# Handing out six PSUM banks by expected release, and moving the middle of an output unit of a fused attention and MLP kernel

## The chip, the cores and the metric

The kernel runs on one core of one Trainium2 chip. Its time is what the device takes for one execution, in microseconds (us); the figure given for a kernel is the median of its runs. One further execution was profiled. All readings below are of that one.

## The reference

The input is `x`, 2048 tokens of 576 features, in float32. Two branches are computed from it and mixed by a gate, one value for each token.

```
qkv = x @ wqkv                       # 32 heads of 18
p = softmax(q k^T * 18**-0.5)        # 2048 x 2048 for each head
a = (p @ v) @ wo
y = layernorm(x)                     # no scale, no shift
b = gelu_tanh(y @ w1 + b1) @ w2 + b2 # 576 -> 4608 -> 576
g = sigmoid(sum(x * gate_w))
out = g * a + (1 - g) * b
```

## The kernel before, in words

The order of the instructions on each engine is the order in which the program writes them; nothing reorders them later. Nearly every float32 product is made of three float32r products, of a high and a low part of each operand.

**Opening.** The tokens are transposed on TensorE (`transposed`, L909), projected to q, k and v (`qk_group` L994, `v_group` L1012), and stored. The normed tokens are transposed too (`y_chunk`). In the gaps of this order stand the first maxima (below).

**The loop.** Attention runs by 32 units. A unit is one pair of heads and one half of the queries. It has 16 steps, one for each 128 keys, so the loop has 512 steps. Head 0 of a pair lies in rows 0 to 63 of TensorE's array and head 1 in rows 64 to 127, so that two matmuls, one on each half of the array, can run side by side. Three sorts of attention work are in the loop:

- *Maxima* (`s1_round`, L227 and L229). A matmul of 128 queries by 512 keys, and on VectorE a maximum over it. One round is two matmuls, one for each head. There are 32 rounds a unit, done for the unit after the current one. `s1_finish` makes of them rows that are stored into the query tile by eight small DMAs (`qa<-mr`).
- *Scores for exp* (`s2`, L310 and L312). A matmul of 128 keys by 512 queries, with the negated maximum as extra rows, and the exponential on ScalarE. A call of `s2` is two matmuls, one for each head. Each step has two calls.
- *Sums* (`pv`, L338). The exponentials times the values, four narrow matmuls side by side, accumulated in one PSUM bank over the 16 steps of a unit. `pv` is called once in two or three steps. At a unit's end VectorE copies the bank out (`oe`, L351).

The MLP branch is a generator, `mlp`, that the loop draws from between two calls of `s2` (`fill`, which takes one `atom`, up to the next cut). It has two kinds of pieces. `h_pair` makes two blocks of the hidden layer, 27 pairs of matmuls of 512 columns (L582), of which the GELU is made on ScalarE, VectorE and GpSimd. `out_pair` makes one *output unit*: 24 pairs of matmuls of 288 columns (L714, 64 rows each) for 128 tokens, whose two results VectorE adds to an accumulator (L688). There are 144 output units.

In the first twelve pairs of an output unit, the *first turn*, array half 0 adds into one bank and half 1 into the other. In the second turn the halves change banks. Before the first product of the second turn the program waits on the semaphore `turn`, which the last products of the first turn raise. The middle of the unit is this place.

A call of `s2` takes a round of maxima with it where `loop_round` gives one: the order is then score, maximum, maximum, score, on halves 0, 1, 0, 1. Where it gives none, its two matmuls are *woven* (`weave`) with the MLP's: score on half 0 beside two MLP products on half 1, and then the reverse. `lend_round` takes a round ahead of its call, as two maxima alone, and marks in `lent` that the next call goes without. `next_round` does a round that no call owes.

**PSUM.** Of the eight banks of 512 float32 columns, two (`ps_w`) belong to the MLP. Two (`ps_s2`) belong to the scores for exp, by turns. Four (`ps_x`) are shared by maxima and sums: three go round for the maxima (`Rotating`, which the opening's transposes use too), and one holds the running sum; when a new sum begins, `Sums` takes the next of the three and gives back the old one.

Of the kernel before, what the change touches and what calls it, by code (L numbers as in the profile page):

```python
# [29 lines left out]
G = 4  # L30
# [23 lines left out]
AHEAD = 3200.0  # L54
BARE = NSTEP - LEAD - NT
# [5 lines left out]
def gated_mix_kernel(ctx: ExitStack, tc: tile.TileContext, x, wqkv, wo, w1, b1, w2, b2, gate_w, out):  # L61
# [37 lines left out]
    class Rotating:  # L99
# [6 lines left out]
    class Sums:  # L106

        def tile(self, *args, **kw):
            i = turn_x.pop(0)
            turn_x.append(held_x[0])  # L110
            held_x[0] = i
            return ps_x[i].tile(*args, **kw)

    ps_s1 = Rotating()
    ps_o = Sums()
# [100 lines left out]
    def s1_round(u, r):  # L216


        t, kb = (r % 8, r // 8) if u == 0 else divmod(r, 4)
        if r == 0:  # L220
            M4[u] = asm.tile([P, 2, 8, 4], F32, name="m4")
        qa, ka = QA[u % 3], k_tile(UNITS[u][0])

        def head(h):
            r0 = 64 * h
            ps = psum(ps_s1)
            nc.tensor.matmul(ps, qa[r0:r0 + 54, t * P:(t + 1) * P], ka[r0:r0 + 54, kb * TB:(kb + 1) * TB],  # L227
                             start=True, stop=True)
            nc.vector.tensor_reduce(M4[u][:, h, t, kb:kb + 1], ps, axis=AX.X, op=ALU.max)  # L229
        return head  # L230
# [53 lines left out]
    def weave(order, heads, need):  # L284

        if not held:
            for h in order:
                heads[h]()
            return
# [9 lines left out]
    def s2(u, kc, qb, around, ns):  # L299
# [7 lines left out]
        def head(h):  # L307
            ps = psum(ps_s2)
# [3 lines left out]
            nc.scalar.activation(ring(n)[:, qb, h], ps, AF.Exp, scale=SCALE)  # L312

# [13 lines left out]
    def pv(n0, n1):  # L327

        flush()
        for c in range(n0, n1):  # L330
            u, k = divmod(c, NT)
            if k == 0:
                OB[u] = psum(ps_o)
            v = VT[UNITS[u][0] % 2]
            for qb in range(2):
                for h in range(2):
                    r = 32 * (2 * h + qb)
                    nc.tensor.matmul(OB[u][r:r + 32, :], v[:, k, 19 * h:19 * h + 32], ring(c)[:, qb, h, :],  # L338
                                     start=(k == 0), stop=(k == NT - 1))
            if k == NT - 1:  # L340
                o_store(u, OB.pop(u))
# [4 lines left out]
    def o_store(u, ps):  # L346
# [4 lines left out]
        nc.vector.tensor_copy(oe, ps)  # L351
        cols = slice(2 * pair * DH, 2 * (pair + 1) * DH)
# [53 lines left out]
    def mlp():  # L406
# [63 lines left out]
        def split(table, key, pool, shape, raw, src, scr, then):  # L470

            def first():
# [3 lines left out]
                nc.scalar.activation(t[:, 0], src(), AF.Copy)  # L476
                bg.insert(0, (any_time, lambda: second(t), queue))
# [64 lines left out]
        def free_pool():  # L542

            if rounds:
                return ps_w
            turns[0] += 1
            return (ps_s1, ps_w)[(turns[0] - 1) // 2 % 2]

        def banks(q):

            if q % 2 and not looped[0]:
                return [psum(ps_s2) for _ in range(2)]
            return [psum(free_pool()) for _ in range(2)]

        def h_pair(q, last, inner=False):
# [8 lines left out]
            ps = banks(q)  # L564
# [14 lines left out]
            for k, (w_, s_, c) in enumerate(slots):  # L579
# [3 lines left out]
                weave((0, 1), [partial(head, 0), partial(head, 1)], 1)  # L583
# [23 lines left out]
            nc.scalar.activation(zs[0], ps[0], AF.Identity, bias=b[0])  # L607
            for h in (1, 0):
# [52 lines left out]
                def second(w, parts):  # L661
                    aside[0] = slot[0]
                    nc.scalar.activation(w, w, AF.Tanh, scale=GC1)
                    if early:
# [3 lines left out]
                def square(w=w, z=z):  # L668
                    aside[0] = slot[0]
                    nc.scalar.activation(w, z, AF.Square)  # L670
                    if early:
# [6 lines left out]
        def out_pair(i, t, acc):  # L678
# [11 lines left out]
            ps = [psum(free_pool()) for _ in range(2)]  # L690
            ends = {7, 15} if piece[0] == 0 else cuts(24, max(1, 3 - piece[0]))
            k = 0
            for turn in range(2):
                if turn == 1:
                    flush()
                if turn == 1 and bare:
                    add(ps, g == 0)
                    ps = [psum(free_pool()) for _ in range(2)]
# [5 lines left out]
                for j in ORDER:  # L704
# [5 lines left out]
                    for h_, p_ in ((hh, 0), (hh, 1), (hl, 0)):  # L710
# [13 lines left out]
                        weave((0, 1) if turn == 0 else (1, 0), [partial(head, 0), partial(head, 1)], 2)  # L724
# [9 lines left out]
            add(ps, g == 0 and not bare)  # L734
            if g == NG - 1:
# [123 lines left out]
    with ExitStack() as a:  # L859
# [46 lines left out]
        def transposed(tb, c):  # L906
            ps = psum(ps_s1)
            for t in range(4):
                nc.tensor.transpose(ps[:, t * P:(t + 1) * P], x_view(tb)[:, t, c * P:(c + 1) * P], ident)  # L909
            return ps  # L910
# [119 lines left out]
        def v_chunk(tb, stage):  # L1030
# [16 lines left out]
            for c in cs_:  # L1047
                for cy in (c, 4 + c) if c < 4 else (8,):
                    ps = psum(ps_s1)
                    for t in range(4):  # L1050
                        nc.tensor.transpose(ps[:, t * P:(t + 1) * P], x_view(tb)[:, t, 64 * cy:64 * cy + P], ident)
                    nc.scalar.activation(made[0][:, cy, :], ps, AF.Copy)
# [22 lines left out]
        for tb in range(NB):  # L1075
# [3 lines left out]
            for g, (fn, args) in enumerate(work):  # L1079
# [49 lines left out]
                if tb == 2 and g == 13:  # L1129
                    ps = psum(ps_s1)  # L1130
                    nc.tensor.transpose(ps[:, :NFC], b1r, ident[:NFC, :NFC])
                    nc.vector.tensor_copy(b1t, ps[:, :NFC])
                for _ in range(ROUNDS[tb](g)):
# [7 lines left out]
    ps_s2 = ctx.enter_context(tc.tile_pool(name="ps_s2", bufs=2, space=PSUM))  # L1141
# [15 lines left out]
    def out_proj():  # L1157
# [125 lines left out]
        for b in range(NB):  # L1283
            per = 4 if b == 2 else 1
            res = {}
            for i0 in range(0, 8, per):
# [4 lines left out]
                for cut_ in (range(4), range(4, 5)):  # L1291
                    for t, n in tiles:
                        tok = slice(t * P, (t + 1) * P)
                        cs = slice(n * ND, (n + 1) * ND)
                        if 0 in cut_:
                            ps[t, n] = psum((ps_s1, ps_w)[banks % 2])
                            banks += 1
                        for c in cut_:
# [3 lines left out]
                            flush()  # L1302
                            for k, (s_, w_) in enumerate(prods):
# [7 lines left out]
                        if n == 0:  # L1311
                            res[t] = io.tile([P, D], F32, name="res")
                        nc.vector.scalar_tensor_tensor(res[t][:, cs], ps[t, n][:, :ND], gate[:, tt:tt + 1], BT[tt // 2][:, t % 2, cs],
                                                       op0=ALU.mult, op1=ALU.add)
                        yield 122.5
# [113 lines left out]
```

## Time and profile before

| what | us |
|---|---|
| median of three runs (range) | 2239.19 (2237.62 to 2239.44) |
| the profiled execution | 2240.08 |
| its span, from the first to the last instruction | 2238.3 |
| TensorE (PE) busy | 2222.0 |
| VectorE (DVE) busy | 1651.7 |
| ScalarE (ACT) busy | 1440.2 |
| GpSimd (POOL) busy | 949.1 |

The profiled execution took 1.8 us more than its span, and lies 0.9 us above the median. PE is busy through nearly the whole span, but this share must be read with care: a matmul counts as busy from its start to a modelled end, and matmuls on the two halves of the array overlap. A half that stands still while the other one works, or while the last product drains, shows as no idle time. So the starts of matmuls are what is to be read here, against the pace at which they follow each other where nothing holds them up.

### The profile page before, as it was taken

How to read it: one execution, taken by the hardware profiler on the slowest of the kernel's cores; microseconds unless marked ns; L12 is line 12 of the kernel's file. 1: busy time of each engine (PE TensorE's matmuls, PEld its weight loads, DVE VectorE, ACT ScalarE, POOL GpSimd, SP SyncE). 2: the span in 40 equal slices, each digit the busy share in tenths (PEclk: the TensorE clock that was granted, in tenths of full speed). 3: DMA queues.
4: the chain of work that ended last, by engine and by line, in shares of the span. 5: the costliest groups of instructions: out<-in, count | busy, mean ns of one | idle time of the engine just before them, and what ended most of it. 6: DMA issues, size and time to landing. Idle time of an engine off the chain costs nothing.

```text
span 2238.3 us, 51156 instructions
## 1 busy us (share of the span) xinstructions
PE 2222.0 (99%) x20569; PEld 1619.8 (72%) x20569; DVE 1651.7 (74%) x2887; ACT 1440.2 (64%) x2719; POOL 949.1 (42%) x936
## 2 busy tenths in 40 slices
PE   8999999999999999999999999999999999999999
PEld 7878677777767776677776776776777677777668
DVE  5675777777777777777777777777777777787834
ACT  4223677777776666666666666666766667666771
POOL 4002466666664444444445444444534444434420
PEclk9999999999999999999999999999999999999999
DMA  7755654536485424242273424233563333333355
GB/s 237 259 190 181 204 171 140 168 133 177 149 228 184 123 100 122 99 143 96 99 184 138 123 99 123 100 125 119 138 182 113 133 114 102 113 93 105 122 175 179
DMA packets 163411, 323.62 MB, mean 145 GB/s; under 512 B 59838, under 2 KB 86370, under 8 KB 152338
## 3 DMA queue, kind: packets, MB, share of 16 engines
q1 hardware_dynamic: 159462, 313.60, 44.0%
q10 hardware_dynamic: 3712, 6.75, 0.8%
q8 instruction: 162, 2.65, 0.5%
q14 instruction: 75, 0.61, 0.1%
HBM read 229.07 MB, written 95.16 MB: 145 GB/s over the span
## 4 chain that ended last, share of the span: by engine, by line
PE 96%; DVE 1%; DMA 1%; POOL 1%; ACT 1%; SPq 0%; issue 0%; ACTq 0%; DVEq 0%; POOLq 0%
PE ps L338 21%; PE ps L714 20%; PE ps L582 20%; PE ps L310 14%; PE ps L227 11%; PE ps L994 5%; PE ps L1012 2%; PE ps L1304 2%; PE ps L909 1%; PE ps L1043 0%; DMA x<-in_A_x_dram 0%; DVE m L229 0%; POOL zz L180 0%; DMA ot_scr<-dn_scr 0%; DMA dn_scr<-dn 0%
## 5 line engine op out<-in xcount | busy, mean ns | idle before, releaser
L229 DVE TENSOR_REDUCE m<-ps 128x1 f32<-128x512 f32 x2048 | 1302.7, 684 | 327.1 <-PE ps L227 273.5
L312 ACT ACTIVATE p<-ps 128x512 f32<-128x512 f32 x1080 | 586.7, 596 | 290.7 <-PE ps L227 185.4
L310 PE MATMUL ps<-qa,ka 56*128 56x512 f32 x2048 | 701.0, 411 | 3.2 <-DMA qa<-mr 2.6
L312 ACT ACTIVATE ring<-ps 128x512 f32<-128x512 f32 x968 | 525.8, 596 | 270.9 <-PE ps L227 175.9
L227 PE MATMUL ps<-ka,qa 54*128 54x512 f32 x2048 | 648.5, 415 | 1.2 <-DVE big L925 0.8
L714 PE MATMUL ps<-w,hh 64*128 64x288 f32 x4352 | 530.3, 296 | 0.7 <-ACT z L607 0.6
L582 PE MATMUL ps<-big,w 64*128 64x512 f32 x3888 | 516.4, 392 | 0.1
L310 PEld LDWEIGHTS ps<-qa,ka 56*128 56x128 f32 x2048 | 360.8, 185 | 213.3 <-issue 75.0
L180 POOL TENSOR_SCALAR zz<-zz 128x512 f32<-128x512 f32 x272 | 169.1, 622 | 759.3 <-ACT zz L670 730.3
L582 PEld LDWEIGHTS ps<-big,w 64*128 64x128 f32 x3888 | 379.4, 185 | 74.8 <-ACT vt L1023 0.3
L714 PEld LDWEIGHTS ps<-w,hh 64*128 64x128 f32 x4352 | 421.1, 186 | 14.2 <-ACT z L607 1.0
L180 POOL TENSOR_TENSOR zz<-zz,z 128x512 f32<-128x512 f32 x280 | 361.8, 1292 | 36.5 <-ACT zz L672 10.5
L714 PE MATMUL ps<-w,hl 64*128 64x288 f32 x2176 | 363.5, 292 | 0.0
L227 PEld LDWEIGHTS ps<-ka,qa 54*128 54x128 f32 x2048 | 339.4, 185 | 29.3 <-DVE m L229 5.7
L338 PE MATMUL ps<-p,vt 128*32 128x512 f32 x2160 | 265.2, 598 | 0.1
L714 PEld LDWEIGHTS ps<-w,hl 64*128 64x128 f32 x2176 | 248.4, 185 | 1.1
L338 PE MATMUL ps<-ring,vt 128*32 128x512 f32 x1936 | 238.3, 598 | 0.0
L180 POOL TENSOR_TENSOR w<-x,w 128x576 fp32r<-128x576 f32 (+1 forms) x34 | 68.4, 2013 | 273.8 <-ACT w L476 247.7
L180 POOL TENSOR_TENSOR hl<-zz,hh 128x512 fp32r<-128x512 f32 x134 | 174.3, 1301 | 15.2 <-ACT hh L633 4.4
L688 DVE SCALAR_TENSOR_TENSOR x<-ps,x 128x288 f32<-128x288 f32 x268 | 110.1, 453 | 85.7 <-PE ps L714 76.9
L338 PEld LDWEIGHTS ps<-p,vt 128*32 128x32 f32 x2160 | 57.9, 109 | 127.0 <-issue 125.4
L338 PEld LDWEIGHTS ps<-ring,vt 128*32 128x32 f32 x1936 | 52.1, 109 | 112.9 <-issue 112.7
(120 smaller groups left out, 1470.0 us busy)
## 6 DMA issues: line engine op xcount, KB each, us to landing
w<-w_scr SPq DMA_DIRECT2D x54, 1152.0 KB
w<-w_scr SPq DMA_DIRECT2D x108, 576.0 KB
w_scr<-w SPq DMA_DIRECT2D x18, 1152.0 KB
w_scr<-w SPq DMA_DIRECT2D x36, 576.0 KB
qa<-qk_scr SPq DMA_DIRECT2D x192, 72.0 KB
ka<-qk_scr SPq DMA_DIRECT2D x90, 144.0 KB
big<-y_scr SPq DMA_DIRECT2D x48, 256.0 KB
x<-in_B_w_dram SPq DMA_DIRECT2D x34, 288.0 KB
```

The costliest lines, as they stand in the source:

```text
L180: fn(*args, **kw)
L227: nc.tensor.matmul(ps, qa[r0:r0 + 54, t * P:(t + 1) * P], ka[r0:r0 + 54, kb * TB:(kb + 1) * TB], start=True, stop=True)
L229: nc.vector.tensor_reduce(M4[u][:, h, t, kb:kb + 1], ps, axis=AX.X, op=ALU.max)
L310: nc.tensor.matmul(ps, ka[r0:r0 + 56, kc * P:(kc + 1) * P], qa[r0:r0 + 56, qb * TB:(qb + 1) * TB], start=True, stop=True)
L312: nc.scalar.activation(ring(n)[:, qb, h], ps, AF.Exp, scale=SCALE)
L338: nc.tensor.matmul(OB[u][r:r + 32, :], v[:, k, 19 * h:19 * h + 32], ring(c)[:, qb, h, :], start=(k == 0), stop=(k == NT - 1))
L582: nc.tensor.matmul(ps[h], wt[w_][r, c, :], Y[s_][r, c, :], start=(k == 0), stop=(k == 26))
L688: nc.vector.scalar_tensor_tensor(dst, ps[nn][:, :ND], 0.5, b2b[:, cs[nn]] if base else dst, op0=ALU.mult, op1=ALU.add)
L714: mm = nc.tensor.matmul(ps[nn][:, :ND], h_[r, tok], w_[p_][r, cs[nn]], start=(k == 0 or bare and k == 3 * G), stop=(k == 6 * G - 1 or bare ...
L994: nc.tensor.matmul(ps, w_[:, c, ms], big[:, s_, :], start=(k == 0), stop=(k == len(prods) - 1))
L1012: nc.tensor.matmul(ps[:, :ND], big[:, s_, tok], w_[:, c, cs], start=(k == 0), stop=False)
L1304: nc.tensor.matmul(ps[t, n][:, :ND], OT[b][3][:, s_, tok], w_part(w_, c)[:, cs], start=(c == 0 and k == 0), stop=(c == 4 and k == 1))
```

## The change

The program keeps a rough clock for PE, ACT and DVE while it is written out. Six banks (four `ps_x`, and two more once the loop begins) are one pool. A matmul for scores, maxima or sums, and in some places a pair of the MLP's, takes the bank whose release is expected first (`Earliest`). After the reading instruction is written, `let_go` sets when that bank is expected back: the reader's clock, plus a fixed time. `ps_w` stays. In the opening the pool has four banks, all of them in use.

In an output unit that begins at a cut (`piece[0] == 0`) while rounds of maxima remain, here `folded`, the cuts fall behind pairs 6 and 12 in place of 7 and 15. The first cut's call of `s2` goes without maxima, the second one's call, with maxima, falls on the middle, so that no round is lent there. The round that the first call passed over is done alone behind pair 18. (Each of the first four output units has one round more, as before.)

```diff
+DRAIN = 330.0
+MAX_NS = 580.0
+EXP_NS = 490.0
...
-    ps_x = [ctx.enter_context(tc.tile_pool(name=f"ps_x{i}", bufs=1, space=PSUM)) for i in range(NS1 + 1)]
-    turn_x = list(range(NS1))
-    held_x = [NS1]
...
+    bank_x = [ctx.enter_context(tc.tile_pool(name=f"ps_x{i}", bufs=1, space=PSUM)) for i in range(4)]
+    free_at = [0.0] * 4
+    pe_t, act_t, dve_t = [0.0], [0.0], [0.0]
+
+    class Earliest:
+
         def tile(self, *args, **kw):
-            i = turn_x.pop(0)
-            turn_x.append(i)
-            return ps_x[i].tile(*args, **kw)
+            i = min(range(len(bank_x)), key=lambda b: free_at[b])
+            pe_t[0] = max(pe_t[0], free_at[i])
+            taken[0] = i
+            free_at[i] = 1e12
+            return bank_x[i].tile(*args, **kw)
...
+    def let_go(i, clock, ns):
+
+        clock[0] = max(clock[0], pe_t[0] + DRAIN) + ns
+        free_at[i] = clock[0]
...
             nc.vector.tensor_reduce(M4[u][:, h, t, kb:kb + 1], ps, axis=AX.X, op=ALU.max)
+            pe_t[0] += 116.0
+            let_go(taken[0], dve_t, MAX_NS)
...
             nc.scalar.activation(ring(n)[:, qb, h], ps, AF.Exp, scale=SCALE)
+            pe_t[0] += 116.0
+            let_go(taken[0], act_t, EXP_NS)
...
         nc.vector.tensor_copy(oe, ps)
+        let_go(bank, dve_t, 620.0)
...
             ends = {7, 15} if piece[0] == 0 else cuts(24, max(1, 3 - piece[0]))
+            folded = piece[0] == 0 and not bare
+            if folded:
+                ends = {6, 12}
...
                     if 3 * G not in ends:
                         lend_round()
                     turned[0] += 2
                     nc.tensor.wait_ge(turn_sem, turned[0])
...
-                        if k == 5 * G and extra[0]:
-                            extra[0] -= 1
+                        if folded and k == 6:
+                            if extra[0]:
+                                extra[0] -= 1
+                            else:
+                                lent[0] = 1
+                        if folded and k == 18:
                             next_round()
...
-    ps_s2 = ctx.enter_context(tc.tile_pool(name="ps_s2", bufs=2, space=PSUM))
+    for i in range(4, 6):
+        bank_x.append(ctx.enter_context(tc.tile_pool(name=f"ps_x{i}", bufs=1, space=PSUM)))
+        free_at.append(pe_t[0])
```

**On PE.** The first piece is an output unit as 134 of the 144 stand in the program before, from the call behind pair 7 to a little past the middle. L714 is a product of the output unit, L310 a score for exp, L227 a maximum; `ps` is the bank written, `w`, `hh` and `hl` are the MLP's operands.

```order
L310 MATMUL ps<-qa_111,ka_112 128x512 [waits Activation_49]
L227 MATMUL ps<-ka_112,qa_109 128x512 [waits DVE_49] x2
L310 MATMUL ps<-qa_111,ka_112 128x512 [waits Activation_49]
L714 MATMUL ps<-w_9841,hh 128x288 x2
L714 MATMUL ps<-w_9841,hl 128x288 x2
L714 MATMUL ps<-w_9839,hh 128x288 x4
L714 MATMUL ps<-w_9839,hl 128x288 x2
L227 MATMUL ps<-ka_112,qa_109 128x512 [waits DVE_49] x2
L714 MATMUL ps<-w_9835,hh 128x288 [waits turn]
L714 MATMUL ps<-w_9835,hh 128x288 x3
L714 MATMUL ps<-w_9835,hl 128x288 x2
```

The two lent maxima, and nothing else, stand between the last products of the first turn and the product that waits for them.

The second piece is the same place of a like unit in the changed program, where the lines have other numbers: L751 is the output unit's product, L320 the score, L234 the maximum.

```order
L751 MATMUL ps<-w_9236,w_8897 128x288 x6
L320 MATMUL ps<-qa_110,ka_113 128x512 [waits DVE_49]
L234 MATMUL ps<-ka_112,qa_111 128x512 [waits Activation_49]
L234 MATMUL ps<-ka_112,qa_111 128x512 [waits DVE_49]
L320 MATMUL ps<-qa_110,ka_113 128x512 [waits Activation_49]
L751 MATMUL ps<-w_9208,hh 128x288 [waits turn]
L751 MATMUL ps<-w_9208,hh 128x288 x3
L751 MATMUL ps<-w_9208,hl 128x288 x2
L751 MATMUL ps<-w_9223,hh 128x288 x4
L751 MATMUL ps<-w_9223,hl 128x288 x2
L234 MATMUL ps<-ka_112,qa_111 128x512 [waits Activation_49] x2
L751 MATMUL ps<-w_9251,w_8897 128x288 x6
```

Two scores and two maxima now stand at the turn, and the two maxima without scores have moved six pairs behind it, where no product waits for a semaphore. A score can now wait for DVE and a maximum for ACT, since banks pass from one kind to the other.

**On ACT.** The next two pieces are exponentials (L312, then L322) of the loop, each written into one of the ring's tiles (`p`, `ring`), with what they wait for. First the program before:

```order
L312 ACTIVATE p<-ps 128x512 [waits PE_49] x2
L663 ACTIVATE zz<-zz 128x512 [waits Pool_49]
L312 ACTIVATE p<-ps 128x512 [waits PE_49] x4
L312 ACTIVATE ring_2271<-ps 128x512 [waits PE_49] x4
L312 ACTIVATE p<-ps 128x512 [waits PE_49] x8
```

and the changed one:

```order
L322 ACTIVATE ring_2282<-ps 128x512 [waits PE_49] x4
L322 ACTIVATE p<-ps 128x512 [waits PE_49] x2
L322 ACTIVATE p<-ps 128x512 [waits PE_49,Activation_49]
L322 ACTIVATE p<-ps 128x512 [waits PE_49]
L322 ACTIVATE p<-ps 128x512 [waits PE_49,Activation_49]
L322 ACTIVATE p<-ps 128x512 [waits PE_49]
L322 ACTIVATE p<-ps 128x512 [waits PE_49,Activation_49] x2
```

Some exponentials (488 of 2048) have a second wait, for ACT's own earlier write of the same ring tile. Before, that was known from the score's wait for ACT; it no longer is where the score's bank came back from DVE.

More of the change, by code (lines that the diff above doesn't have):

```diff
@@ L282, in flush, with weave @@
             tail()
-    def weave(order, heads, need):
+    def weave(order, heads, need, ns):
+        pe_t[0] += ns
         if not held:
@@ L476, in first @@
                 nc.scalar.activation(t[:, 0], src(), AF.Copy)
+                engine(act_t, 900.0)
                 bg.insert(0, (any_time, lambda: second(t), queue))
@@ L540, in mlp, with pair_of_banks, wide_banks, give_back @@
         turns = [0]
[L542 to L547, printed above, removed]
+        def pair_of_banks(own):
+            if own:
+                return [psum(ps_w) for _ in range(2)], ()
+            tiles, ids = [], []
+            for _ in range(2):
+                tiles.append(psum(ps_x))
+                ids.append(taken[0])
+            return tiles, ids
         def banks(q):
             if q % 2 and not looped[0]:
-                return [psum(ps_s2) for _ in range(2)]
-            return [psum(free_pool()) for _ in range(2)]
+                return pair_of_banks(False)
+            return wide_banks()
+        def wide_banks():
+            if rounds:
+                return pair_of_banks(True)
+            turns[0] += 1
+            return pair_of_banks(turns[0] % 2 == 0)
+        def give_back(ids):
+            for b in ids:
+                let_go(b, dve_t, 480.0)
         def h_pair(q, last, inner=False):
@@ L563, in h_pair @@
             del W1[q]
-            ps = banks(q)
+            ps, ids = banks(q)
             if q == 0:
@@ L607, in h_pair @@
             nc.scalar.activation(zs[0], ps[0], AF.Identity, bias=b[0])
+            engine(act_t, 690.0)
+            give_back(ids)
             for h in (1, 0):
@@ L663, in second @@
                     nc.scalar.activation(w, w, AF.Tanh, scale=GC1)
+                    engine(act_t, 640.0)
                     if early:
@@ L670, in square @@
                     nc.scalar.activation(w, z, AF.Square)
+                    engine(act_t, 640.0)
                     if early:
@@ L697, in out_pair @@
                     add(ps, g == 0)
-                    ps = [psum(free_pool()) for _ in range(2)]
+                    give_back(ids)
+                    ps, ids = wide_banks()
                 elif turn == 1:
@@ L1284, in out_proj @@
             per = 4 if b == 2 else 1
-            res = {}
+            res, own = {}, {}
             for i0 in range(0, 8, per):
@@ L1295, in out_proj @@
                         if 0 in cut_:
-                            ps[t, n] = psum((ps_s1, ps_w)[banks % 2])
+                            ps[t, n] = psum((ps_x, ps_w)[banks % 2])
+                            own[t, n] = None if banks % 2 else taken[0]
                             banks += 1
@@ L1314, in out_proj @@
                                                        op0=ALU.mult, op1=ALU.add)
+                        if own[t, n] is not None:
+                            let_go(own[t, n], dve_t, 480.0)
                         yield 122.5
```

43 lines of the change are left out of this document (22 added, 21 removed).

## The prediction

> **What bounds the kernel now.** I read the page first, then the busy time in chosen stretches, then the starts of matmuls one by one.
>
> ```profile
> span 2238.3 us, 51156 instructions
> PE 2222.0 (99%) x20569; PEld 1619.8 (72%) x20569; DVE 1651.7 (74%) x2887; ACT 1440.2 (64%) x2719; POOL 949.1 (42%) x936
> ...
> PE 96%; DVE 1%; DMA 1%; POOL 1%; ACT 1%; SPq 0%; issue 0%; ACTq 0%; DVEq 0%; POOLq 0%
> ```
>
> The first two lines and the chain that ended last say that TensorE sets the time. They leave it 16 us of idle time in all, so that no wait seems worth removing. But busy is not the same as working, so I took one output unit and cut it at its middle. The columns after the stretch are its length, then busy time and instructions of each engine.
>
> ```profile
> core 0: us, PE busy (x) PEld busy (x) DVE busy (x) ACT busy (x) POOL busy (x), PEclk, DMA share, GB/s
> 805.84:807.90 2.06, 2.06 (x30) 2.04 (x27) 2.06 (x5) 1.74 (x4) 0.00 (x0) 1.00 0.10 19
> 807.90:810.68 2.78, 2.78 (x36) 2.50 (x32) 2.17 (x5) 1.62 (x4) 0.00 (x0) 1.00 0.45 125
> 1000.00:1500.00 500.00, 500.00 (x4936) 354.12 (x4934) 384.71 (x662) 337.97 (x646) 224.36 (x237) 1.00 0.39 125
> ```
>
> PE is busy for the whole of both halves, at full clock. The first half holds 12 product pairs, one score pair and one maxima pair. The second holds 12 product pairs, the lent maxima, a woven score pair, and a last call of two pairs. What these should take is read from the starts in that unit (timeline of PE alone: start, length, what):
>
> ```profile
> 805.60 0.40 PE L310 MATMUL ps<-qa,ka 56*128 56x512 f32 x1
> 805.84 0.43 PE L714 MATMUL ps<-w,hh 64*128 64x288 f32 x4
> ...
> 806.76 0.40 PE L227 MATMUL ps<-ka,qa 54*128 54x512 f32 x1
> ...
> 807.24 0.32 PE L714 MATMUL ps<-w,hh 64*128 64x288 f32 x2
> ...
> 807.90 0.39 PE L227 MATMUL ps<-ka,qa 54*128 54x512 f32 x1
> ...
> 807.98 0.49 PE L227 MATMUL ps<-ka,qa 54*128 54x512 f32 x1
> ...
> 808.16 0.40 PE L714 MATMUL ps<-w,hh 64*128 64x288 f32 x1
> 808.16 0.45 PE L714 MATMUL ps<-w,hh 64*128 64x288 f32 x2
> ...
> 810.36 0.39 PE L310 MATMUL ps<-qa,ka 56*128 56x512 f32 x1
> ...
> 810.68 0.64 PE L338 MATMUL ps<-p,vt 128*32 128x512 f32 x4
> ```
>
> From 805.84 to 806.76 stand seven product pairs: 0.92 / 7 = 0.131 us for one. From 806.76 to 807.24 stand two pairs of 512 columns: 0.24 us for one, as from 805.60 to 805.84. The sums (L338) begin 0.32 us after the last score, 0.08 more than its 0.24. So the first half should take 12 x 0.131 + 2 x 0.24 = 2.05 us, and takes 2.06. The second should take 12 x 0.131 + 4 x 0.24 + 0.08 = 2.61 us, and takes 2.78. The loss is all behind the turn. There the second maximum starts 0.08 us after the first (it waits for a bank that DVE has to read), the product with the wait on `turn` starts at 808.16, and the next product of the other half behind it. The first maximum left its half of the array free at about 807.90 + 0.24 = 808.14, with nothing to run until those products are let in.
>
> Is this one unit typical? These are the first product and the first sum of the three others of its group (the pair 805.84 and 810.68 above is the fourth):
>
> ```profile
> 791.08 0.43 PE L714 MATMUL ps<-w,hh 64*128 64x288 f32 x4
> ...
> 796.11 0.64 PE L338 MATMUL ps<-p,vt 128*32 128x512 f32 x4
> ...
> 798.54 0.43 PE L714 MATMUL ps<-w,hh 64*128 64x288 f32 x4
> ...
> 803.41 0.64 PE L338 MATMUL ps<-ring,vt 128*32 128x512 f32 x4
> ...
> 813.11 0.43 PE L714 MATMUL ps<-w,hh 64*128 64x288 f32 x4
> ...
> 817.98 0.64 PE L338 MATMUL ps<-ring,vt 128*32 128x512 f32 x4
> ```
>
> The four take 5.03, 4.87, 4.84 and 4.87 us, on the mean 4.90. Undisturbed, a unit is 24 x 0.131 + 6 x 0.24 + 0.08 = 4.66 us. The loss is 0.24 us on the mean, 0.18 at the least, 0.37 at the most.
>
> **The change part by part.**
>
> *The turn.* The orders of both programs have 134 output units of the one pattern, replaced by the other; work and number of `pv` calls are the same. In the new order the two array halves have 2 x 0.24 = 0.48 us of scores and maxima to stream between the last product of the first turn and the one that waits for it; before, they had one pair, 0.24 us, of which the second began late. In the row above the waiting product starts 0.26 us after the lent maxima do, so 0.48 us covers the wait with 0.2 to spare. What is queued behind this wait on PE is the whole kernel, so what it gives up is time. I take 0.20 us a unit: more than the least of the four, less than their mean, because the slowest (5.03) also has tanh passes on ACT, which stay. 134 x 0.20 = 26.8 us. The ends: nothing, if a new wait stands at the turn or at the moved maxima, and 134 x 0.24 = 32 us.
>
> *What is late next: the banks.* How long a bank is held is read where both readers were idle (start, length, engine):
>
> ```profile
> 999.02 0.39 PE L310 MATMUL ps<-qa,ka 56*128 56x512 f32 x1
> 999.03 0.62 PE L227 MATMUL ps<-ka,qa 54*128 54x512 f32 x2
> ...
> 999.45 0.60 ACT L312 ACTIVATE ring<-ps 128x512 f32<-128x512 f32 x1 [0.55 <-PE ps L227]
> 999.49 0.69 DVE L229 TENSOR_REDUCE m<-ps 128x1 f32<-128x512 f32 x1 [0.34 <-PE ps L227]
> ```
>
> A score holds its bank 1.03 us (to 1000.05), a maximum 1.15 us (to 1000.18). Now the new unit by the prices above, from its first product: call without maxima at 0.79, call at the turn at 1.81, lone maxima at 3.08, last call at 4.10 and 4.34, sums at 4.66. By the program's bank numbers the shortest reuse, at 1.26 us of distance, is of three kinds: a score at the turn takes the bank of the first woven score, the second lone maximum that of a score or a maximum at the turn, and the last score that of the first lone maximum. Against 1.03 us there are 0.23 to spare, against 1.15 only 0.11. Does DVE keep up?
>
> ```profile
> 806.01 3.72 DVE L229 TENSOR_REDUCE m<-ps 128x1 f32<-128x512 f32 x6
> 810.33 0.82 DVE L688 SCALAR_TENSOR_TENSOR x<-ps,x 128x288 f32<-128x288 f32 x2 [0.61 <-PE ps L714]
> ```
>
> Six maxima in a row take 3.72 us, 0.62 each. At the turn the first can start at 1.81 + 0.46 = 2.27, the second ends its turn by 2.27 + 2 x 0.62 = 3.51, and the lone ones are ready at 3.08 + 0.46 = 3.54: no queue. So the bank comes back at 3.08 + 1.15 = 4.23, and the last score wants it at 4.34. Cost: nothing, with 0.11 us of cover. If DVE lags by one maximum the wait is 0.62 - 0.11 = 0.51 us a unit (rivals).
>
> *The opening.* Here the order stays, and the ring of three banks becomes a pool of four. Two of the places where a maximum waits for a bank:
>
> ```profile
> 135.53 0.49 PE L227 MATMUL ps<-ka,qa 54*128 54x512 f32 x1
> ...
> 136.81 0.49 PE L227 MATMUL ps<-ka,qa 54*128 54x512 f32 x1 [0.79 <-DVE big L925]
> ...
> 141.19 1.09 PE L227 MATMUL ps<-ka,qa 54*128 54x512 f32 x2
> ...
> 141.79 0.18 PEld L227 LDWEIGHTS ps<-ka,qa 54*128 54x128 f32 x1 [0.42 <-DVE m L229]
> ```
>
> The second maximum starts 1.28 and 0.60 us after the first, on the other half of the array, which could start at once. With a fourth bank it takes one that was used a tile earlier. The most is 1.9 us; the least is nothing, if DVE's queue only passes the wait on. I take 1.5, nearer the upper end, since the first wait is for a transpose's reader (`big` L925) and not for DVE's queue of maxima.
>
> *ACT.* Of the exponentials 488 get a second wait. The nearest row is that of the GELU's first step, which has such waits:
>
> ```profile
> L607 ACTq EVENT_SEMAPHORE  x68: 17/17/38, 307.8 to 2113.9; - x68
> ```
>
> At 0.017 us each they come to 8.3 us of ACT's time. ACT is busy 338 of 500 us in the loop, so I cost them at nothing; if that cover is gone, all 8.3 us. Each makes a score's bank come back 0.02 us later, out of 0.23.
>
> *The maxima's lead.* The round passed over at the first cut comes later by up to one call; four calls and the sums stand in 7.30 us (805.84 less 798.54), so that is 1.8 us. Last maximum of a unit, its rows' DMAs, first score that needs them:
>
> ```profile
> 1880.66 0.57 PE L227 MATMUL ps<-ka,qa 54*128 54x512 f32 x2
> ...
> 1887.62 5.57 SPq L134 DMA_DIRECT2D qa<-mr  x8
> ...
> 1897.10 0.39 PE L310 MATMUL ps<-qa,ka 56*128 56x512 f32 x1
> ```
>
> The last DMA is issued by 1893.19, and 3.9 us are left to land. Less 1.8, and less what a faster loop takes from it (under 0.5), 1.6 us remain. These eight stay in their order on SP's queue, so a later maximum holds up what stands behind them there (loads of q, k, weights) by the same 1.8 us at most, ahead of uses that are whole units away. Cost: nothing; at the worst the rows land late by the 1.8 us for 31 units, 56 us, which the 3.9 us argue against.
>
> *DMAs, GpSimd, the other lines* are neither added nor removed.
>
> The sum, against the profiled execution: 2240.1 - 26.8 - 1.5 = 2211.8 us. The median of the runs is 0.9 us below that execution, so I give 2211.
>
> **The rivals.**
>
> *Half of it.* The turn is freed, but the lone maxima or the last score wait by about 0.10 us a unit, as the second lent maximum does now by 0.08. For it: the cover is only 0.11 us, and the program's clock for DVE leaves out the 0.82 us of the two additions. Against: these come before the maxima at the turn, and DVE is idle 115 of 500 us. 134 x 0.10 = 13.4 us gained, 1.5 in the opening: 2225.
>
> *Slower: exponentials wait for DVE.* Before, no score waited for DVE. Now the last score of a unit needs the bank of the first lone maximum. If DVE lags there by one maximum, 0.62 us, the wait is 0.51 us a unit, and 134 x (0.51 - 0.20) = 41.5 us are lost: 2280. It decides from a lag of 0.11 + 0.20 = 0.31 us on. For it: DVE works in the order written, so any GELU or softmax step in front adds its whole length. Against: such a step stands in the unit's first half or in hidden-layer stretches, and the additions leave DVE about 1 us free in a unit (8 x 0.62 + 0.82 = 5.78 of 7.30).
>
> *No change: the readers of PSUM are the pace.* If DVE and ACT empty the banks as fast as they can, a stall removed on PE comes back as a wait for a bank: 2240. For it: DVE is busy without a gap in the first half of the unit above (2.06 of 2.06). Against: 2.17 of 2.78 in the second, and 385 of 500 in the loop. The Trainium skill, "TensorEngine Tiling (Array Packing)", section "Performance Considerations", has this as a rule: tiling speeds up TensorE but not the emptying of PSUM, which may then become the bottleneck. By that rule the whole 28 us would not come. The trace agrees only for stretches of some 2 us, not over a unit.
>
> **How the numbers follow.** The forecast has 0.70: the loss at the turn stands in all four units, and its cause leaves the place. Its own range is 2205 to 2220, from the full 32 us and the opening's 1.9 to a loss of 0.15 us removed per unit. Half of it has 0.13 (2220 to 2231), no change 0.08 (which takes in an order that doesn't act as told), slower 0.07, and more than the full loss 0.02. A measurement of this kernel tells about 0.2%, 4.5 us, from no change. So faster has 0.70 + 0.13 + 0.02 = 0.85, same 0.08, slower 0.07. Leaving out no change, slower and a little at each end, the range is 2203 to 2229.
>
> **What would show it.** Right: an output unit takes 4.66 to 4.72 us from its first product to the sums; the product that waits on `turn` starts with its partner, 0.24 us after the last score; the second maximum of the opening's pairs starts with the first. PE's busy share stays 99%. Wrong: a gap in front of the lone maxima, or before the last score of the unit with DVE as its releaser; units of 4.8 us and more; the first score of a unit waiting for `qa<-mr`; or stretches of hidden-layer pairs that grow, where I expect none.

## The result, and the profile after

The changed kernel takes 2215.1 us (median of five runs, 2215.0 to 2215.5), against 2239.1 us before in the runs beside it: a ratio of 0.9896, with a 95% interval of 0.9885 to 0.9907. The forecast was 2211. The profiled execution took 2215.03 us, its span 2213.1 us.

```profile
span 2213.1 us, 51656 instructions
...
PE 2196.4 (99%) x20569; PEld 1599.6 (72%) x20569; DVE 1644.7 (74%) x2887; ACT 1436.3 (65%) x2719; POOL 949.1 (43%) x936
```

These two lines of the page show the same 20569 matmuls and the same busy share of PE, in 25 us less. As before, the share tells nothing; the starts do. This is the timeline of PE (start, length, what) for one output unit of the usual length:

```profile
790.68 0.44 PE L751 MATMUL ps<-w,hh 64*128 64x288 f32 x4
...
791.48 0.40 PE L320 MATMUL ps<-qa,ka 56*128 56x512 f32 x1
...
792.51 0.40 PE L320 MATMUL ps<-qa,ka 56*128 56x512 f32 x1
792.53 0.61 PE L234 MATMUL ps<-ka,qa 54*128 54x512 f32 x2
792.76 0.40 PE L320 MATMUL ps<-qa,ka 56*128 56x512 f32 x1
792.98 0.44 PE L751 MATMUL ps<-w,hh 64*128 64x288 f32 x4
...
793.78 0.41 PE L234 MATMUL ps<-ka,qa 54*128 54x512 f32 x2
...
795.07 0.39 PE L320 MATMUL ps<-qa,ka 56*128 56x512 f32 x1
795.39 0.64 PE L350 MATMUL ps<-ring,vt 128*32 128x512 f32 x4
```

The unit lasts from 790.68 to 795.39, 4.71 us. The first products of the second turn start at 792.98, 0.22 us after the last score of the call, together on both halves. The two lone maxima start together at 793.78.

Over all 134 units of the pattern (first product to first sum, from the records' starts) the mean went from 4.888 to 4.728 us, the median from 4.863 to 4.704. This is 0.160 us a unit, 21.5 us over the 134. The loop's part from the first product of the fifth output unit to that of the 139th is this, before and after:

```profile
311.48 0.30 PE L714 MATMUL ps<-w,hh 64*128 64x288 f32 x2
...
2116.12 0.40 PE L714 MATMUL ps<-w,hh 64*128 64x288 f32 x1
```

```profile
309.15 0.30 PE L751 MATMUL ps<-w,hh 64*128 64x288 f32 x2
...
2092.97 0.40 PE L751 MATMUL ps<-w,hh 64*128 64x288 f32 x1
```

1804.64 against 1783.82 us: 20.8 us gained. So the stretches between the units, those with hidden-layer pairs above all, give back 0.7 us, where the prediction expected no growth. Ahead of the first of these starts the changed kernel gained 2.3 us, and behind the second one 2.0.

### The profile page after: what moved, and what is told of

Its sections match the earlier page's. It is cut to its first block, busy times and chain, and to the rows that moved or that the text cites. A ratio compares the mean times of both kernels' runs of the same rounds, so it can differ in the third digit from the quotient of the medians.

```text
span 2213.1 us, 51656 instructions
## 1 busy us (share of the span) xinstructions
PE 2196.4 (99%) x20569; PEld 1599.6 (72%) x20569; DVE 1644.7 (74%) x2887; ACT 1436.3 (65%) x2719; POOL 949.1 (43%) x936
## 5 line engine op out<-in xcount | busy, mean ns | idle before, releaser
L322 ACT ACTIVATE p<-ps 128x512 f32<-128x512 f32 x1080 | 582.6, 596 | 283.4 <-PE ps L234 188.8
L322 ACT ACTIVATE ring<-ps 128x512 f32<-128x512 f32 x968 | 523.2, 596 | 259.5 <-PE ps L234 186.5
L320 PE MATMUL ps<-qa,ka 56*128 56x512 f32 x2048 | 685.9, 409 | 4.5 <-DMA qa<-mr 2.6
L234 PE MATMUL ps<-ka,qa 54*128 54x512 f32 x2048 | 625.6, 409 | 0.9 <-DVE big L968 0.7
L320 PEld LDWEIGHTS ps<-qa,ka 56*128 56x128 f32 x2048 | 358.4, 185 | 212.0 <-DVE m L236 130.8
L751 PE MATMUL ps<-w,hh 64*128 64x288 f32 x4352 | 491.2, 293 | 0.9 <-ACT z L636 0.8
L751 PEld LDWEIGHTS ps<-w,hh 64*128 64x128 f32 x4352 | 418.1, 186 | 22.1 <-ACT z L636 1.2
L751 PE MATMUL ps<-w,hl 64*128 64x288 f32 x2176 | 340.7, 293 | 0.0
L234 PEld LDWEIGHTS ps<-ka,qa 54*128 54x128 f32 x2048 | 318.2, 186 | 23.1 <-issue 3.6
L751 PEld LDWEIGHTS ps<-w,hl 64*128 64x128 f32 x2176 | 236.9, 186 | 0.0
L1037 PE MATMUL ps<-big,wqk 128*128 128x512 f32 x504 | 123.5, 400 | 0.0
```

The costliest lines, as they stand in the source:

```text
L320: nc.tensor.matmul(ps, ka[r0:r0 + 56, kc * P:(kc + 1) * P], qa[r0:r0 + 56, qb * TB:(qb + 1) * TB], start=True, stop=True)
L751: mm = nc.tensor.matmul(ps[nn][:, :ND], h_[r, tok], w_[p_][r, cs[nn]], start=(k == 0 or bare and k == 3 * G), stop=(k == 6 * G - 1 or bare ...
L1037: nc.tensor.matmul(ps, w_[:, c, ms], big[:, s_, :], start=(k == 0), stop=(k == len(prods) - 1))
```

## The experiments

Six of the kernels are best compared by where in the unit its tiles start. The table gives medians over the 134 units, in us from the unit's first product ("maxima" and "next" are the two array halves), and the mean unit.

| kernel | maxima ahead of `turn` | first products | next products | last tile | sums | mean unit |
|---|---|---|---|---|---|---|
| before | 2.061, 2.142 | 2.324, 2.478 | 2.568, 2.615 | 4.542 | 4.863 | 4.888 |
| no turn | 2.068, 2.148 | 2.300, 2.434 | 2.483, 2.566 | 4.553 | 4.880 | 4.902 |
| pool only | 2.061, 2.111 | 2.330, 2.350 | 2.563, 2.569 | 4.504 | 4.831 | 4.847 |
| pool, no turn | 2.062, 2.112 | 2.298, 2.353 | 2.433, 2.488 | 4.428 | 4.754 | 4.771 |
| changed | 2.067, 2.074 | 2.298, 2.308 | 2.435, 2.442 | 4.375 | 4.704 | 4.728 |
| changed, no turn | 2.069, 2.074 | 2.300, 2.308 | 2.436, 2.443 | 4.378 | 4.707 | 4.732 |

(In the two changed kernels the second column is the pair that is last before the products: a maximum and a score.) In all six the sums start 0.32 to 0.33 us after the last tile.

### Each half of the change alone

The order without the pool. The banks stay as they were before the change; only the cuts and the places of the maxima are the new ones:

```diff
+            folded = piece[0] == 0 and not bare
+            if folded:
+                ends = {6, 12}
...
+                        if folded and k == 6:
...
+                                lent[0] = 1
+                        if folded and k == 18:
+                            next_round()
```

> The kernel before, with the new cuts and the moved maxima alone; its banks stay as they were (two for scores by turns, three for maxima, one held). Theory A, order and pool need each other: at the turn the second score wants its bank 2.05 us into the unit, and of two banks by turns it gets that of the second woven score, whose exponential ends at about 1.05 + 0.44 + 0.23 (queue) + 0.60 = 2.32. So a unit waits some 0.3 us and is 5.0 us long against 4.89 before: slower by 134 x 0.1 = 13 us, 2252. Rival B, the order is the gain: 2239 - 21 = 2218. Rival C, the pool is the gain: 2239, no change.

Measured: 2267.6 us, ratio 1.0128 (1.0113 to 1.0143). Slower, as theory A said, but by 29 us instead of 13. The unit takes 5.107 us. PE and PEld (weight loads), in a usual unit:

```profile
528.95 0.49 PE L310 MATMUL ps<-qa,ka 56*128 56x512 f32 x1
529.04 0.65 PE L227 MATMUL ps<-ka,qa 54*128 54x512 f32 x2
529.44 0.49 PE L310 MATMUL ps<-qa,ka 56*128 56x512 f32 x1
```

```profile
529.44 0.18 PEld L310 LDWEIGHTS ps<-qa,ka 56*128 56x128 f32 x1 [0.19 <-ACT ring L312]
```

The second score at the turn waits until ACT has read the second woven score (it starts 0.49 us after the first one, not 0.24). That is the wait that was expected. By the medians this score is 0.30 us later in the unit than in the changed kernel (2.371 and 2.074). What follows on its half of the array is later by 0.40: the half's first product (2.708 and 2.308; in this kernel it is the third by starts), the second lone maximum (3.504 and 3.105), the last score (4.770 and 4.375). So 0.10 us more is lost right behind the wait, and all of it is carried to the unit's end. A second wait for a bank isn't seen there, though the second lone maximum starts 0.22 us after the first:

```profile
530.35 0.40 PE L227 MATMUL ps<-ka,qa 54*128 54x512 f32 x1
530.44 0.29 PE L717 MATMUL ps<-w,hl 64*128 64x288 f32 x1
530.57 0.40 PE L227 MATMUL ps<-ka,qa 54*128 54x512 f32 x1
```

It starts 0.13 us after a product, the undisturbed pace, in this unit and in the median one. The rows also show that matmuls on different halves need not start in the order in which they are written: the program writes both maxima behind pair 18, and yet one product of that pair starts behind the first maximum, in 133 of the 134 units. That nothing reorders the instructions, as the description of the kernel has it, holds for the lists that the program writes, and not for these starts. The new order alone is no gain at all; it needs the banks.

The pool without the order:

```diff
-    ps_x = [ctx.enter_context(tc.tile_pool(name=f"ps_x{i}", bufs=1, space=PSUM)) for i in range(NS1 + 1)]
+    bank_x = [ctx.enter_context(tc.tile_pool(name=f"ps_x{i}", bufs=1, space=PSUM)) for i in range(4)]
...
-            ps = psum(ps_s2)
+            ps = psum(ps_x)
```

> The changed kernel with the old cuts, the lent maxima and their old places; the pool of six by expected release stays. Theory A: the turn keeps its loss, and only the second lent maximum no longer waits its 0.08 us; the opening's 2.5 us and the tail's 2 are kept. 2239 - 4.5 - 134 x (0 to 0.08) = 2224 to 2235, I take 2232. Rival B (order): 2239 to 2235. Rival C (pool): 2215.

Measured: 2230.7 us, ratio 0.9965 (0.9952 to 0.9978), in the range of theory A. But of the 0.08 us between the two lent maxima only 0.03 goes with the wait for the bank (2.142 to 2.111). Most of the other 0.05 is older than the turn: behind the unit's first call the products of the two halves start at 1.40 and 1.44 us in the old order, with and without the pool, where both start at 1.30 in the changed kernel.

### The wait on `turn` alone

The kernel before, with the halves kept in their banks in the second turn:

```diff
-                    turned[0] += 2
-                    nc.tensor.wait_ge(turn_sem, turned[0])
...
-                            nn = h ^ turn
+                            nn = h
```

> The kernel before, in which the halves of the array keep their banks in the second turn, so that no product has to wait there (the second turn's partial products land in the other result: the output is not the reference's). Work and order are the same. It prices the wait on turn alone, with the bank wait of the second lent maximum (0.08 us) left in. Theory A: of some 0.19 us lost at the turn 0.08 stay, 134 x 0.11 = 14 us faster: 2225. Rival, the loss is the wait for DVE's bank alone: no change, 2239.

Measured: 2241.0 us, ratio 1.0009 (1.0000 to 1.0019). The expectation was wrong by 16 us: the wait that was held to be the main loss is taken away, and nothing is gained. The same edit on top of the pool:

> The pool of six banks with the old order, and without the turn: in the second half of an output unit the array halves keep their banks (so that half of the products are added to the other result), and nothing waits on `turn` or raises it. Theory A, two waits that overlap at the middle of the unit: the bank of the second lent maximum (gone with the pool) and `turn` (gone here). The pool alone gave 2230.7 and the missing turn alone 2241.0 against 2238.8; with both gone the unit falls by about as much as in the changed kernel, 0.16 us, and the time by 134 x 0.16 + 2.5 for the opening: 2215, in 2212 to 2219. Rival, the new order is itself what gains (two maxima fewer in a row, other places of the calls): no more than the pool alone, 2229 to 2233.

Measured: 2221.0 us, ratio 0.9921 (0.9907 to 0.9936). This is 2 us above the range that theory A gave, but with its mechanism: the mean unit gains 0.041 us by the bank alone, loses 0.014 without `turn` alone, and gains 0.117 by both. Two waits lay over each other, and each hid the other. The loads show how. In the program with the pool, with and without `turn`:

```profile
523.24 0.26 PEld L234 LDWEIGHTS ps<-ka,qa 54*128 54x128 f32 x2
523.62 0.30 PEld L748 LDWEIGHTS ps<-w,hh 64*128 64x128 f32 x4
```

```profile
634.63 0.26 PEld L234 LDWEIGHTS ps<-ka,qa 54*128 54x128 f32 x2
634.76 0.48 PEld L746 LDWEIGHTS ps<-w,hh 64*128 64x128 f32 x4
```

The loads for the products start 0.38 us after those for the maxima where `turn` is waited for, and 0.13 us after them where it isn't. By the table the first products are only 0.03 us later with the wait on one half, and no later on the other, but the next pair is 0.13 and 0.08 later, since its loads, 0.18 us each, could not be made ahead either. And in the kernel before without `turn`, a load that waits for a bank does the same:

```profile
579.69 0.39 PEld L227 LDWEIGHTS ps<-ka,qa 54*128 54x128 f32 x2
579.90 0.34 PEld L712 LDWEIGHTS ps<-w,hh 64*128 64x128 f32 x3
```

The second maximum's load waits for its bank, the products' loads stand behind it, and one half's first product starts at 2.434, hardly earlier than with `turn` (2.478). So both waits cost through the same thing, the loads in a row behind them. The Trainium skill, "TensorE: Matmul & The Clock Gate", section "Step-by-step: what each phase is for", says that weight loads are pulled ahead of running matmuls. These rows agree (the load at 634.76 starts together with the first of the two maxima). They also show that behind a wait there is no such lead, and that one more pair pays.

What the order adds to that is 4.771 - 4.728 = 0.043 us, 5.8 us in all. With the old order the second maximum still starts 0.05 us after the first, and one half of the array stays that much behind to the unit's end, where the sums start behind the later one.

Is `turn` still felt in the changed kernel? The same edit there:

> The changed kernel without the turn, again with the second half's products added to the other result. Theory A: in the changed kernel the wait on `turn` is met before it is reached, since 0.46 us of scores and maxima stand between: 2215, in 2213 to 2217. Rival: the wait still holds the product back, or the loads behind it, and is what the unit has over 4.66 us, 0.07 us: 134 x 0.07 = 9 us less, 2206.

Measured: 2214.1 us, ratio 0.9890 (0.9875 to 0.9905), and the last two rows of the table are alike. Theory A holds: the wait is met before it is reached.

### The banks behind the gain

The pool of four in the opening only, as a ring, and the rest as before:

```diff
-    turn_x = list(range(NS1))
-    held_x = [NS1]
+    turn_x = list(range(NS1 + 1))
+    held_x = []
```

> The kernel before with its fourth ps_x bank in the opening's ring until the first sum takes it; the loop keeps three and one. Theory: the opening's 2.5 us (first score of the loop at 247.9 us in the changed kernel against 250.4) come from the fourth bank: 2236.6. Rival, they come from the order of release that the pool works out or from elsewhere: 2239.

Measured: 2237.5 us, ratio 0.9994 (0.9985 to 1.0003), 1.25 us less than before. The interval takes in no change, so the time alone decides nothing. By the starts, 1.3 us are gained between the 31st matmul and the first output unit (in the changed kernel 1.5).

One bank fewer in the loop:

```diff
-    for i in range(4, 6):
+    for i in range(4, 5):
```

> The changed kernel with one bank fewer in the pool once the loop begins: four go round beside the sum's, in place of five. Theory A, each of the last four tiles of a unit then takes the bank of four tiles ago: the last score that of the second lone maximum, whose release lies at 4.80 us of the unit where the score would start at 4.38, and so it waits 0.48 us: 134 x 0.48 = 64 us, 2279, in 2262 to 2295. Rival, the gain is the order's and the shared pool's, and the sixth bank is spare: 2213 to 2219.

Measured: 2331.5 us, ratio 1.0414 (1.0397 to 1.0432). The direction and the named place are right, the size isn't: 116 us instead of 64, with 5.455 us a unit.

```profile
541.03 0.18 PEld L320 LDWEIGHTS ps<-qa,ka 56*128 56x128 f32 x1 [0.30 <-ACT ring L322]
...
543.75 0.18 PEld L320 LDWEIGHTS ps<-qa,ka 56*128 56x128 f32 x1 [0.41 <-DVE m L236]
```

The last score waits for DVE (the second row), as expected. The second score at the turn waits too, for an exponential (the first row), which the expectation left out. The sixth bank is what carries the order.

Six banks, handed out in the order in which they were let go, without the clocks:

```diff
-            i = min(range(len(bank_x)), key=lambda b: free_at[b])
+            i = min(range(len(bank_x)), key=lambda b: given[b])
```

> The changed kernel, with the bank handed out that was let go longest ago by the program's order, instead of the one whose release the clocks expect first; six banks as before. Theory A: the clocks matter only in the units (about 34 of 134) in which a GELU step stands in front on an engine, and there a lone maximum gets the bank of a score of the middle and waits some 0.35 us: 34 x 0.35 = 12 us, 2227, in 2220 to 2234. Rival: six banks are enough in any fair order, 2213 to 2217.

Measured: 2231.7 us, ratio 0.9969 (0.9956 to 0.9981). Theory A holds. The median unit is unchanged (4.708 us). But the first unit of each group of four, in which tanh steps still stand on ACT, takes 5.036 us on the mean, against 4.759 with the clocks. One of them, loads and ACT:

```profile
523.56 0.18 PEld L238 LDWEIGHTS ps<-ka,qa 54*128 54x128 f32 x1 [0.23 <-ACT ring L326]
```

```profile
522.39 0.63 ACT L698 ACTIVATE zz<-zz 128x512 f32<-128x512 f32 x1
522.91 1.08 ACT L326 ACTIVATE ring<-ps 128x512 f32<-128x512 f32 x2
```

A tanh puts the exponentials late, and the lone maximum waits for a bank that one of them reads; the clocks give it another. (Units make up 10.8 of the 16.6 us against the changed kernel; the rest is in the stretches between them and was not followed up.)

### How much DVE may lag

One maximum at the turn is taken twice, or preceded by one over a quarter of its columns:

```diff
+            for _ in range(1 + twice[0]):
+                nc.vector.tensor_reduce(M4[u][:, h, t, kb:kb + 1], ps, axis=AX.X, op=ALU.max)
...
+                        if folded and k == 12:
+                            twice[0] = 1
```

> The changed kernel with one maximum at the middle of each output unit taken twice on VectorE, 0.62 us more there. Theory A, the cover is as thin as reckoned: the bank of the last score in a unit comes back from the first lone maximum 0.15 us before the score starts, where the least seen is 0.05, so that 0.62 less 0.09 becomes a wait: 134 x 0.5 = 67 us, 2282, in 2270 to 2290. Rival: VectorE has idle time in the unit (1.3 of 4.73 us) and takes it up before the banks are wanted: 2215 to 2222.

> The changed kernel with one maximum at the middle of each output unit preceded by one over its first 128 columns, into the same place: a quarter of the columns, an estimated 0.2 to 0.3 us more on VectorE in each unit (a whole one, 0.62 us, cost 0.62 us a unit, 0.12 more than a cover of 0.1 us would leave). Theory A, a cover of 0.1 us is there and the larger loss of the whole maximum came from what a late score does to the sums behind it: 134 x (0.25 - 0.1) = 20 us, 2235, in 2225 to 2243. Rival B, there is no cover, VectorE sets the pace of the unit's second half: 134 x 0.25 = 34 us, 2249, in 2243 to 2256. Rival C, VectorE's idle time takes this much up: 2213 to 2219.

Measured: 2300.9 us, ratio 1.0278 (1.0263 to 1.0294), for the whole one; 2249.9 us, ratio 1.0050 (1.0035 to 1.0065), for the quarter. The whole one is slower than theory A gave it, and the quarter falls to rival B by its time. First the ends of two usual units (PE; whole, then quarter):

```profile
544.02 0.49 PE L235 MATMUL ps<-ka,qa 54*128 54x512 f32 x1
544.61 0.50 PE L323 MATMUL ps<-qa,ka 56*128 56x512 f32 x1
545.04 0.64 PE L353 MATMUL ps<-p,vt 128*32 128x512 f32 x4
```

```profile
536.28 0.40 PE L235 MATMUL ps<-ka,qa 54*128 54x512 f32 x1
536.47 0.50 PE L323 MATMUL ps<-qa,ka 56*128 56x512 f32 x1
536.89 0.62 PE L353 MATMUL ps<-p,vt 128*32 128x512 f32 x2
```

Then DVE's row of maxima and the load of the late score in each of them, and the same of the changed kernel, in the unit shown at the start:

```profile
541.95 3.21 DVE L238 TENSOR_REDUCE m<-ps 128x1 f32<-128x512 f32 x5 [1.02 <-PE ps L235]
...
544.61 0.18 PEld L323 LDWEIGHTS ps<-qa,ka 56*128 56x128 f32 x1 [0.41 <-DVE m L238]
```

```profile
534.20 2.81 DVE L238 TENSOR_REDUCE m<-ps 128x1 f32<-128x128 f32 x5 [1.02 <-PE ps L235]
...
536.47 0.18 PEld L323 LDWEIGHTS ps<-qa,ka 56*128 56x128 f32 x1 [0.23 <-DVE m L238]
```

```profile
792.98 2.52 DVE L236 TENSOR_REDUCE m<-ps 128x1 f32<-128x512 f32 x4 [1.01 <-PE ps L234]
...
794.96 0.18 PEld L320 LDWEIGHTS ps<-qa,ka 56*128 56x128 f32 x1
```

The row takes 2.52 us in the changed kernel, 3.21 with the whole maximum and 2.81 with the quarter: DVE was given 0.69 and 0.29 us. By the medians the last score comes 0.59 and 0.19 us late, so 0.10 us is covered both times. But the sums lose it again: they start 0.42 us after that score, not 0.33. The loads show why. In the changed kernel the load of the last score starts at 794.96, 0.11 us ahead of its matmul. In the two others it starts with the matmul, and the record of the matmul is 0.50 us long and not 0.39. In the usual unit of all three kernels the load starts 0.05 us after DVE has read the first lone maximum. So the load waits for this bank in the changed kernel already: in the 15 units that have one bank more (below) it starts 0.14 us earlier, at 4.134 us of the unit and not 4.274, and the score hardly so. Its lead is all the cover there is, and when it is used up the sums pay for it. Lateness alone does not cost them the 0.10: in the kernel with the order alone the last score starts 0.22 us behind the tile before it, with its load made ahead, and the sums start 0.32 us after it.

So a usual unit, of which there are 119, loses what DVE was given: 0.68 and 0.28 us. The other 15 units lose 0.26 us to the whole maximum and nothing to the quarter. They begin 0.44 us after DVE starts to copy a sum's bank out, and the next sum takes a bank only at their end, so that they have one bank more. DVE has the same row of maxima there (2.81 us), so what is paid in the others is the missing bank, and not a pace of DVE as rival B has it. That the mean unit of the quarter grows by 0.251 us, as that rival counted, is chance: 119 units pay more and 15 pay nothing.

## Why the prediction held, and where its sizes were off

**The turn, 26.8 us predicted, 21.5 measured.** That the loss stands behind the turn and leaves it was right, and the new schedule came out almost as worked out: call without maxima at 0.80 (0.79 predicted), call at the turn 1.83 (1.81), lone maxima 3.10 (3.08), last call 4.14 and 4.37 (4.10 and 4.34), sums 4.70 (4.66). The mis-sized step is the undisturbed unit. Its pairs were priced at 0.131 us, from one run of seven; over all units the first six take 0.798, 0.133 each, and over 24 pairs that alone makes 0.05 us. So 0.20 us a unit was more than there was to take; 0.160 was.

**Its cause.** The prediction named both waits at the turn, the bank of the second maximum and `turn`, but put one price on them together and didn't ask what is left when one goes. The experiments show that it is all of it, or three quarters: 0.041 us of 0.160 goes with the bank alone, none with `turn` alone. It also put the whole 0.08 us between the two lent maxima down to the bank, of which 0.03 was. That the product with the wait starts with its partner came true (2.298 and 2.308), as well as the forecast that nothing else waits there.

**The banks.** The bank of the last score was to be back at 4.23 us, with 0.11 us of cover. Measured: DVE has read it at 4.22, and the cover is 0.10. What the prediction had wrong is the cost of a lag. It took the cover off, so that the slower rival would decide from a lag of 0.31 us on. At 0.29 us it had already decided (2249.9 against 2239.1), because the cover is the lead of the score's weight load, and what it saves at the score is lost at the sums. In the run as it is, that lag doesn't occur, so the forecast stood. It stood nearer to the edge than it said, since the load starts as soon as the bank is back. The rule of the Trainium skill that was weighed there ("TensorEngine Tiling (Array Packing)", section "Performance Considerations": tiling does not speed up the emptying of PSUM) does not bind the changed kernel, but with a quarter of a maximum more it does in the 119 usual units, for the whole of what is added. In the 15 units with a bank to spare it does not.

That DVE has little time left behind the turn can be read off the change's own trace. Its waits ahead of the additions, before and after (total us, times, longest):

```profile
DVE x L688 <- PE ps L714: 82.9, 125, 3.8
```

```profile
DVE x L721 <- PE ps L751: 14.0, 9, 3.6
```

Before, DVE stood idle for the last product of nearly every unit. Now it comes to the additions late in nearly all.

**The opening, 1.5 us predicted.** By the starts from the 31st matmul to the first output unit it is 1.5 (233.6 to 232.2 us), though not all at the places shown:

```profile
134.54 0.49 PE L234 MATMUL ps<-ka,qa 54*128 54x512 f32 x2
139.60 1.09 PE L234 MATMUL ps<-ka,qa 54*128 54x512 f32 x2 [0.67 <-DVE big L968]
```

The first pair now starts together (it was 1.28 us apart), but 0.67 us of this comes back as a wait of the next pair for the same reader (`big`, now L968), which leaves 0.6 us. That next pair still starts 0.60 us apart, since DVE's queue of maxima passes the wait on. The rest came from later pairs, such as the last:

```profile
226.22 1.09 PE L227 MATMUL ps<-ka,qa 54*128 54x512 f32 x2
```

```profile
224.24 0.40 PE L234 MATMUL ps<-ka,qa 54*128 54x512 f32 x2
```

So the sum was right partly by luck: the two places that it was read from give 0.6 us, and pairs that it didn't look at give the rest. A further 1.0 us ahead of the loop is no effect of the change: in the profiled execution of before the 31st matmul started at 14.08 us, in that of after at 13.09, and in those of the ten experiments, with either kind of pool, between 13.01 and 13.62.

**Costed at nothing.** ACT's second waits came as counted, and the first scores of a unit wait for their rows no longer than before (2.6 us in 2 places, then as now):

```profile
L322 ACTq EVENT_SEMAPHORE  x488: 17/17/17, 274.8 to 2156.6; - x163
```

```profile
PE ps L320 <- DMA qa<-mr: 2.6, 2, 1.8
```

The tail, from the 139th output unit on, is 2.0 us shorter, which was not forecast. In the other ten traces it takes between 118.6 and 122.1 us (before 122.2, after 120.2), with no clear order by pool, so I can't say that the change did it. In the medians of the runs, 24.0 us were gained. Units and opening explain 21.5 + 1.5, less the 0.7 given back between the units; 1.7 stays open.

No version beyond the changed kernel is suggested by the runs: its median unit (4.704) is at the price of its parts (4.71 with 0.133 for a pair), and what the slower units add is 134 x 0.024 = 3 us.

## What to carry to other kernels

Two waits that overlap at one place have no prices of their own: taking away one gave 0.04 us a unit or nothing, both 0.12. Before costing an edit that removes a wait, look for the one that is a little shorter beneath it, and for the weight loads that stand in a row behind either. When banks are shared more tightly, measure how late each reader may be, by giving it a little more work, and read when the load behind it starts as well as the matmul. Here the matmul had the 0.10 us of cover that was worked out by hand, but its load had none, and the lag was paid in full.

## What the runs showed of the hardware

- A wait on PE costs more than its own length. With `turn` the first products came 0.03 us later on one half and no later on the other, but the pair behind them 0.13 and 0.08, because the 0.18 us loads of both had to start behind the wait.
- A tile whose weight load had to wait for a bank costs the next full-width step about 0.10 us beyond its lateness: the sums start 0.42 instead of 0.33 us after it (in the pair of experiments on DVE). A tile that was 0.22 us late with its load made ahead cost nothing beyond (0.32, with the order alone).
- The load that waits for a bank starts 0.05 us after DVE has read the bank, in the usual unit of three kernels.
- A half of the array that has fallen behind the other does not catch up within the turn. With the pool and without `turn` it is 0.05 us at the first product (2.298 and 2.353) and 0.07 at the last tiles (4.359 and 4.428).
- Matmuls on different halves do not always start in the order in which they are written: with the order alone, a product written ahead of a maximum started 0.09 us behind it in 133 of 134 units.
- The first 14 us of one and the same opening differ by 1 us between executions: the 31st matmul started at 14.08 us in the kernel before, and at 13.01 and 13.21 in the two kernels with the same opening (the order alone, and the kernel before without `turn`).
